# Opening of a linear-attention stage: sums and masks by halves of heads for two units, u asked first, head copies on GpSimd

## The chip, the cores and the metric

The kernel runs on one core of one Trainium2 chip. The metric is the device time of one execution in microseconds (us); several runs are made and their median is taken. The core's engines work side by side, each through its own queue in order: TensorE (PE: matrix products and transposes; PEld: its weight loads), VectorE (DVE), ScalarE (ACT), GpSimd (POOL) and SyncE (SP, which here only issues transfers). An engine whose next instruction waits does nothing else in the meantime.

## The reference

An attention block with a decaying state runs first, and its output is the input of a mixture-of-experts block. Sizes: batch B = 4, heads H = 8, sequence S = 768, head size D = 48; 3072 tokens of 384 numbers, 8 experts with a hidden size of 1024.

```
state = 0
for t in range(S):
    cur = (u * k_t) outer v_t
    y_t = r_t @ (state + cur)
    state = w * state + k_t outer v_t
x = y as (B*S, H*D)
logits = x @ w_gate; every token goes to one expert, at most N/E tokens each, best logits first
out[tokens of e] = relu(x @ w1[e]) @ w2[e]
```

The `cur` term gives each token's own contribution, the sum over d of r*u*k for each head, times v. It is needed at once by every tile of tokens, and the first steps of the kernel below prepare it.

## The kernel before, in words

**Units.** The attention stage cuts the sequence into 6 chunks of T = 128 tokens; a chunk of one batch element is a unit, 24 units in all, numbered with the batch element running fastest (units 0 to 3 are the first chunk). The program works in pairs of heads: four pairs `a`, each with a first and a second head `z`, on partitions 0 to 47 and 64 to 111. `head(a, z)` names the head; pairs 0 and 1 hold heads 0 to 3, pairs 2 and 3 hold heads 5, 6, 7 and 4. So head 4 is needed behind head 7, and a *head copy* (`again_one`, line 344; from unit 5 on `again`, line 340, for k and r together on VectorE) puts it there in the tile `krs`.

**What a unit needs.** Its k, r and v are loaded by SP (line 336, 192 KB each). `keys` (line 436, GpSimd) multiplies k by the table `wk`. `own` (lines 442 and 443, GpSimd) forms r*k, then times `u_bc`; `own_sum` (line 448, VectorE) sums it over d into `dd`, one number a head. `diagonal` (line 495, ScalarE) writes eight pieces of `AT`, the identity times `dd` of a head. `turn` transposes k and r on TensorE (line 458); the results are scaled or copied to `kT` and `rT` (lines 473 and 477 on VectorE, 475 on ScalarE). `pairs` forms k times r of all heads on TensorE into the PSUM tile `g_ps` (line 504), and VectorE copies those of earlier tokens over the diagonals in `AT` (line 508, `copy_predicated` with `mask`), one instruction for each `z`. `outputs` multiplies `AT` with v on TensorE (line 542), after the state's part (also line 542's helper) from the second chunk on; ScalarE copies the result (line 560). `keep` (lines 521 to 529) updates the state. `rows` transposes a unit's outputs back to rows (line 591), ScalarE copies them (line 598), SP stores them (line 599). `gate` and `logits` follow after each chunk.

**The order** is written out by hand: the whole stage stands in `tc.manual_schedule()`, so each engine runs its instructions as the program names them. Iteration n of the loop in `run` turns unit n + 2, forms the products of unit n + 1, the keys and own products of unit n + 3, and the outputs of unit n; it asks for k and r of unit n + 5 and v of unit n + 4. `krs` has 5 slots, `vts` 6, `AT` 3, `g_ps`, `y_ps`, `kT_ps` and `rT_ps` one each.

**The opening** (`start`, and `run` up to the loop) must in addition build the tables: powers of w on VectorE (lines 381 to 393), products of powers `Q` (line 395, one on GpSimd and one on VectorE), from these `WK` and `WR` on ScalarE (line 422), and `wk`, which is `WK` transposed on TensorE (line 427) and copied (line 431). u is one row, loaded by GpSimd's queue (line 364) behind the identity; a product with a row of ones spreads it over the partitions (line 409) and ScalarE copies it to `u_bc` (line 413). `idle` (line 418) issues transposes that nobody reads. Unit 0 is scaled straight from `Q` ("pieces"), units 1 and 2 by `WK` and `WR`.

After the attention stage come the assignment of tokens and the experts' products, which the change doesn't touch. The first expert's weights are loaded by SP (line 1506) near the end of the attention stage.

Of the kernel before, what the change touches and what calls it, by code (L numbers as in the profile page):

```python
# [10 lines left out]
F32 = mybir.dt.float32  # L11
# [5 lines left out]
ALU = mybir.AluOpType  # L17
AX = mybir.AxisListType
# [3 lines left out]
T = 128  # L22
# [252 lines left out]
class Mild:  # L275
# [65 lines left out]

    def again_one(self, n, x):
        t, HP, H, D = self.krs[:, n % self.NK, x], self.HP, self.H, self.D
        self.nc.scalar.copy(t[:, H, 0:D], t[:, HP, 0:D])

    def start(self):
        nc, HP, H, D = self.nc, self.HP, self.H, self.D
        half = HP // 2
        nc.vector.memset(self.wp, 1.0)
        with nc.allow_non_contiguous_dma(reason="a row to the partitions"):  # L350
            for eng, z, aa, hh in ((nc.sync, 0, slice(0, half), slice(0, HP, 2)),
# [4 lines left out]
                eng.dma_start(self.wp[z * PD:z * PD + D, aa], self.w[hh].rearrange("h d -> d h"))  # L356
        for n, what in ((0, "kr"), (1, "kr"), (0, "v"), (2, "kr"), (1, "v"), (3, "kr"), (2, "v"), (4, "kr"), (3, "v")):
            self.load(n, what)
        make_identity(nc, self.ident)
        nc.vector.memset(self.krs[:, :, :, :, D:PD], 0.0)  # L360
        AB = self.ones8
        nc.vector.memset(AB[:, :, :, :, 0:1], 1.0)
        nc.gpsimd.memset(self.wgp, 0.0)
        nc.gpsimd.dma_start(self.u_row, self.u.rearrange("h d -> (h d)").unsqueeze(0))
        nc.vector.memset(self.one_row, 1.0)
# [27 lines left out]
        nc.vector.reciprocal(AB[:, 1], AB[:, 0])  # L393
        for x, eng in ((0, nc.gpsimd), (1, nc.vector)):
            eng.tensor_mul(self.Q[:, x], AB[:, x, :, 1, :].unsqueeze(3).to_broadcast([128, HP, 9, 8]),
                           AB[:, x, :, 0, 0:8].unsqueeze(2).to_broadcast([128, HP, 9, 8]))
        Q = self.Q.rearrange("p x a i j -> p x a (i j)")
# [40 lines left out]

    def own(self, n):
        nc, H, D = self.nc, self.H, self.D  # L440
        rk = self.pool.tile([128, H, D], F32, name="rk")
        nc.gpsimd.tensor_mul(rk, self.krs[:, n % self.NK, 1, 0:H, 0:D], self.krs[:, n % self.NK, 0, 0:H, 0:D])  # L442
        nc.gpsimd.tensor_mul(rk, rk, self.u_bc)  # L443
        self.live[n].update(rk=rk)

    def own_sum(self, n):
        dd = self.pool.tile([128, self.H], F32, name="dd")
        self.nc.vector.tensor_reduce(out=dd, in_=self.live[n]["rk"], axis=AX.X, op=ALU.add)  # L448
        self.live[n]["dd"] = dd

# [35 lines left out]

    def diagonal(self, n, zs=(0, 1)):
        nc, HP = self.nc, self.HP
        if "AT" not in self.live[n]:
            self.live[n]["AT"] = self.pool.tile([128, 2, HP, T], F32, name="AT", bufs=3)  # L490
        AT, dd = self.live[n]["AT"], self.live[n]["dd"]
        for z in zs:
            for a in range(HP):
                h = self.head(a, z)
                nc.scalar.mul(AT[:, z, a, :], self.ident, dd[:, h:h + 1])  # L495

    def pairs(self, n, between=None):
        nc, HP, D = self.nc, self.HP, self.D
        kT, rT, AT = (self.live[n][x] for x in ("kT", "rT", "AT"))
        g_ps = self.ps.tile([128, 2, HP, T], F32, name="g_ps")  # L500
        for a in range(HP):
            for z in range(2):
                rows = slice(z * PD, z * PD + D)
                nc.tensor.matmul(g_ps[:, z, a, :], kT[rows, a, :], rT[rows, a, :], start=True, stop=True)  # L504
        if between is not None:
            between()
        for z in range(2):
            nc.vector.copy_predicated(out=AT[:, z], mask=self.mask.unsqueeze(1).to_broadcast([128, HP, T]),  # L508
                                      data=g_ps[:, z])

    def keep(self, n):
# [101 lines left out]
    def run(self, step):  # L613
        N, B, C, walk = self.N, self.B, self.C, self.walk
        self.live = {n: {} for n in range(N)}
        self.start()
        u_ps = self.spread_u()
        self.again_one(0, 0)
        k0 = self.keys_turned(0, True)
        self.again_one(0, 1)  # L620
        self.idle(2, "g_ps")
        r0 = self.r_turned(0)
        self.copy_u(u_ps)
        self.own(0)
        self.scaled(0, "k", k0, "pieces")
        self.scaled(0, "r", r0, "pieces")
        self.table(self.WK, "k")
        self.again_one(1, 0)
        self.table(self.WR, "r")
        self.again_one(1, 1)  # L630
        self.idle(2, "g_ps")
        k1 = self.keys_turned(1, True, walk.ps, "few")
        wk_ps = self.wk_turned()
        r1 = self.r_turned(1, walk.ps, "counts")
        self.wk_table(wk_ps)
        self.scaled(1, "k", k1, self.WK)
        self.own_sum(0)
        self.diagonal(0, (0,))
        self.again_one(2, 0)
        self.diagonal(0, (1,))  # L640
        self.again_one(2, 1)
        self.scaled(1, "r", r1, self.WR)
        self.own(1)
        self.keys(0)
        self.own_sum(1)
        nc, AB = self.nc, self.ones8
        nc.vector.tensor_mul(self.chunk, AB[:, 0, :, 1, 8], AB[:, 0, :, 1, 8])
        self.pairs(0)
        self.diagonal(1)
        self.own(2)  # L650
        chores = walk.constants()
        for n in range(N):
            self.load(n + 5, "kr")
            self.load(n + 4, "v")
            if n == 2:
                self.gate_weights()
            soon, split, full = n <= B, 0 < n < 3, n >= B and n % B == 0
            halves = ((0,), (1,)) if split or full else ((0, 1), ())
# [1221 lines left out]
```

## Time and profile before

| What | us |
|---|---|
| median of 3 runs (398.03 to 398.3) | 398.09 |
| profiled execution | 397.39 |
| its span | 395.7 |
| TensorE busy in the span | 381.1 |
| ScalarE busy | 162.0 |
| GpSimd busy | 138.4 |
| unit 0's k asked / turned on TensorE | 1.89 / 5.27 |
| unit 0's outputs on TensorE | 14.93 to 16.02 |
| copies of the outputs of units 0, 1, 2, 3, 4 (line 560) | 17.83, 21.20, 25.13, 30.22, 36.32 |
| the same of units 5, 6 | 41.02, 45.60 |
| last unit's copy | 124.70 |

In the lines of the profile, a timeline row gives the start, the duration, the engine, the line of the kernel, the operation, what is written from what, the shape, the count, and in brackets how long the engine had been idle and who released it. A row "x8" merges eight instructions, and its duration is that of all of them. The copies of line 560 serve as milestones, one for each unit.

### The profile page before, as it was taken

To read this page: it belongs to the slowest core of one execution; us is meant where nothing else is said; L and a number is where in the kernel's file an instruction comes from. 1 tells how busy PE (TensorE), PEld (TensorE's weight loads), DVE (VectorE), ACT (ScalarE), POOL (GpSimd) and SP (SyncE) were. 2 spreads that over 40 slices of the span, in tenths; PEclk is the share of its full clock that TensorE was granted. 3 is DMA by queue.
4 is the path that set the end of the run, shared out by engine and by line. 5 is a ranking of instruction groups with operands and counts; after the bars stand their busy time and mean duration, and the time that the engine had idled before them with its cause. 6 is when DMAs were issued, how large, how long until landed. Compare 5 with 4: busy or idle time off the path is not lost. (4 is left out here: it accounts for less than half of the span.)

```text
span 395.7 us, 8692 instructions
## 1 busy us (share of the span) xinstructions
PE 381.1 (96%) x3243; PEld 289.3 (73%) x3243; DVE 266.9 (67%) x934; ACT 162.0 (41%) x429; POOL 138.4 (35%) x173
## 2 busy tenths in 40 slices
PE   7899999999999999999999999999999999999993
PEld 5678888888877765587578569558757856966991
DVE  6755777576885677897839819979578663952630
ACT  4998888888873312222222122121222222222130
POOL 7888877666732013032121120302303211040020
PEclk9999999999999999999999999999999999999998
DMA  9999999898692155371460650109209173380010
GB/s 120 156 183 200 200 173 205 156 169 157 117 342 81 42 200 217 96 282 42 160 239 16 214 210 2 60 0 333 87 21 354 59 275 131 92 308 2 2 61 27
DMA packets 95331, 57.29 MB, mean 145 GB/s; under 512 B 77232, under 2 KB 89520, under 8 KB 95280
## 3 DMA queue, kind: packets, MB, share of 16 engines
q1 hardware_dynamic: 91936, 47.21, 47.7%
q0 software_dynamic: 3104, 9.44, 6.8%
q8 instruction: 27, 0.44, 0.5%
q14 instruction: 24, 0.20, 0.2%
q10 hardware_dynamic: 240, 0.00, 0.0%
HBM read 47.20 MB, written 9.44 MB: 143 GB/s over the span
## 5 line engine op out<-in xcount | busy, mean ns | idle before, releaser
L1541 PE MATMUL h_ps<-xT,w 128*128 128x384 f32 (+1 forms) x384 | 120.7, 467 | 0.6 <-ACT xT L1529 0.6
L1541 PEld LDWEIGHTS h_ps<-xT,w 128*128 128x128 f32 x384 | 66.4, 190 | 38.1 <-issue 2.5
L1543 ACT ACTIVATE hid<-h_ps 128x384 f32<-128x384 f32 (+1 forms) x64 | 29.7, 465 | 91.1 <-PE h_ps L1541 85.1
L495 ACT ACTIVATE AT<-ident,dd 128x128 f32<-128x128 f32 x192 | 59.6, 391 | 1.9 <-DVE dd L448 1.8
L1513 POOL DMA_INDIRECT xg<-x_rows,tok x22 | 22.4, 1017 | 95.6 <-PE h_ps L1541 32.1
L1637 POOL DMA_INDIRECT out_dram<-o_all,to x16 | 17.9, 1120 | 94.6 <-DVE o_all L1625 62.2
L508 DVE COPY_PREDICATED AT<-mask,g_ps 128x512 f32<-128x512 uint8 x48 | 32.6, 733 | 12.1 <-PE g_ps L504 10.6
L1620 ACT COPY res<-p_ps 128x384 f32<-128x384 f32 (+2 forms) x28 | 13.3, 474 | 60.5 <-PE p_ps L1616 60.5
L1643 PE MATMUL o_ps<-w,hid 128*128 128x384 f32 x96 | 33.1, 488 | 0.0
L504 PE MATMUL g_ps<-rT,kT 48*128 48x128 f32 x384 | 27.9, 284 | 0.7 <-DVE AT L508 0.6
L436 POOL TENSOR_TENSOR kss<-krs,wk 128x384 f32<-128x384 f32 x24 | 24.3, 1015 | 8.0 <-DVE krs L340 5.5
L504 PEld LDWEIGHTS g_ps<-rT,kT 48*128 48x128 f32 x384 | 23.4, 187 | 4.0 <-PE unread_ps L418 0.5
L542 PE MATMUL y_ps<-AT,vts 128*64 128x128 f32 x384 | 25.7, 276 | 0.0
L443 POOL TENSOR_TENSOR rk<-rk,u_bc 128x384 f32<-128x384 f32 x24 | 24.2, 1007 | 1.9
L442 POOL TENSOR_TENSOR rk<-krs 128x384 f32<-128x384 f32 x24 | 24.5, 1020 | 0.2 <-DMA krs<-in_r_dram 0.2
L1643 PEld LDWEIGHTS o_ps<-w,hid 128*128 128x128 f32 x96 | 17.2, 190 | 9.5 <-issue 0.2
L542 PEld LDWEIGHTS y_ps<-AT,vts 128*64 128x64 f32 x384 | 20.6, 137 | 1.2 <-issue 0.7
L1616 PE MATMUL p_ps<-T,S 128*128 128x192 f32 x120 | 20.9, 328 | 0.0
L1593 DVE TENSOR_TENSOR H<-hid 128x512 f32<-128x512 f32 x12 | 7.9, 686 | 19.1 <-ACT hid L1543 19.1
L1616 PEld LDWEIGHTS p_ps<-T,S 128*128 128x128 f32 x120 | 19.6, 190 | 0.1
L932 DVE TENSOR_TENSOR own<-counts,same 128x64 f32<-128x64 f32 x21 | 4.7, 222 | 21.7 <-PE counts L944 21.6
L1616 PE MATMUL p_ps<-w,hid 128*128 128x192 f32 (+1 forms) x112 | 19.0, 316 | 0.0
(303 smaller groups left out, 694.0 us busy)
## 6 DMA issues: line engine op xcount, KB each, us to landing
w<-in_moe_w_dram SPq DMA_DIRECT2D x18, 1536.0 KB, 10.2
krs<-in_k_dram SPq DMA_DIRECT2D x24, 192.0 KB, 4.0
krs<-in_r_dram SPq DMA_DIRECT2D x24, 192.0 KB, 4.7
vts<-in_v_dram SPq DMA_DIRECT2D x24, 192.0 KB, 4.7
x_rows<-xr SPq DMA_DIRECT2D x24, 192.0 KB, 3.2
xg<-x_rows,tok POOLq DMA_INDIRECT x22, 4.4
out_dram<-o_all,to POOLq DMA_INDIRECT x16, 2.8
out_dram<-o_sb,to POOLq DMA_INDIRECT x5, 3.0
```

What stands on the lines that cost most here:

```text
L436: self.nc.gpsimd.tensor_mul(self.kss[:, n % self.NS].rearrange("p (g h) d -> p g h d", g=2)[:, :, :, 0:D], src, self.wk.rearrange("p (g h) ...
L442: nc.gpsimd.tensor_mul(rk, self.krs[:, n % self.NK, 1, 0:H, 0:D], self.krs[:, n % self.NK, 0, 0:H, 0:D])
L443: nc.gpsimd.tensor_mul(rk, rk, self.u_bc)
L495: nc.scalar.mul(AT[:, z, a, :], self.ident, dd[:, h:h + 1])
L504: nc.tensor.matmul(g_ps[:, z, a, :], kT[rows, a, :], rT[rows, a, :], start=True, stop=True)
L508: nc.vector.copy_predicated(out=AT[:, z], mask=self.mask.unsqueeze(1).to_broadcast([128, HP, T]), data=g_ps[:, z])
L542: nc.tensor.matmul(yv[q * PD:(q + 1) * PD, o // 2, o % 2, :], lhsT, rhs, start=(o // 2, q) not in seen, stop=stop, skip_group_check=True)
L1513: nc.gpsimd.indirect_dma_start(out=xg[:, c, :], out_offset=None, in_=x_dram[0:within, :], in_offset=bass.IndirectOffsetOnAxis(ap=tok[:, c: ...
L1541: nc.tensor.matmul(h_ps[:, 0:m], w1[:, f, ts(j, 128)], xT[:, f, 0:m], start=(f == 0), stop=(f == KD - 1))
L1543: nc.scalar.activation(hid[:, j, 0:m], h_ps[:, 0:m], AF.Relu)
L1616: nc.tensor.matmul(ps[:, q, :], left[a][:, j, :], right[b][:, j, :], start=(j == 0), stop=(j == KF // 2 - 1))
L1643: nc.tensor.matmul(o_ps, hid[:, j, ts(c, 128)], w2[:, j, :], start=(j == 0), stop=(j == KF - 1))
```

## The change

It edits only the attention stage's opening and the placing of some instructions in its first five iterations.

- The load of u is issued on GpSimd's queue before the identity is made there, not behind it.
- Unit 2's k and r are asked ahead of unit 0's v, and so on down the list; inside the loop v is asked for unit n + 3, not n + 4.
- Both `Q` products are on VectorE.
- `own(0)` multiplies k by u first, then by r. For units 0 and 1 the second product of `own`, the sum, the diagonal and the mask are issued in two halves of heads (heads 0 to 3 and 4 to 7; a masked half covers pairs 0 and 1, or 2 and 3, with both `z`).
- Unit 0's first half of the diagonal comes between the two tables; its second half comes after `wk`. `wk` is turned after k and r of unit 1, ahead of unit 0's products. Unit 0's and unit 1's masks are interleaved with unit 1's sums.
- Unit 2's sum (`own_sum(2)`) and the chunk's factor come after unit 1's masks; before, the sum stood ahead of `pairs(1)` and the factor ahead of `pairs(0)`.
- The head copies of units 1 to 7 are on GpSimd (`gpsimd.tensor_copy`); for units 3 to 7 they stand directly before the `keys` and the `own` that use the same unit. Unit 0's stay on ScalarE.
- `own(2)` comes before `keys(0)`. One more idle transpose is issued ahead of unit 1's turn.

```diff
@@ again_one, start
-    def again_one(self, n, x):
+    def again_one(self, n, x, copy=None):
         t, HP, H, D = self.krs[:, n % self.NK, x], self.HP, self.H, self.D
-        self.nc.scalar.copy(t[:, H, 0:D], t[:, HP, 0:D])
+        (copy or self.nc.scalar.copy)(t[:, H, 0:D], t[:, HP, 0:D])
...
-        for n, what in ((0, "kr"), (1, "kr"), (0, "v"), (2, "kr"), (1, "v"), (3, "kr"), (2, "v"), (4, "kr"), (3, "v")):
+        for n, what in ((0, "kr"), (1, "kr"), (2, "kr"), (0, "v"), (3, "kr"), (1, "v"), (4, "kr"), (2, "v")):
             self.load(n, what)
+        nc.gpsimd.dma_start(self.u_row, self.u.rearrange("h d -> (h d)").unsqueeze(0))
         make_identity(nc, self.ident)
...
-        nc.gpsimd.dma_start(self.u_row, self.u.rearrange("h d -> (h d)").unsqueeze(0))
...
-        for x, eng in ((0, nc.gpsimd), (1, nc.vector)):
-            eng.tensor_mul(self.Q[:, x], ...
+        for x in range(2):
+            nc.vector.tensor_mul(self.Q[:, x], ...
@@ own, own_sum, diagonal, pairs
-    def own(self, n):
+    def own(self, n, u_first=False):
         nc, H, D = self.nc, self.H, self.D
+        k, r = (self.krs[:, n % self.NK, x, 0:H, 0:D] for x in range(2))
         rk = self.pool.tile([128, H, D], F32, name="rk")
-        nc.gpsimd.tensor_mul(rk, self.krs[:, n % self.NK, 1, 0:H, 0:D], self.krs[:, n % self.NK, 0, 0:H, 0:D])
-        nc.gpsimd.tensor_mul(rk, rk, self.u_bc)
+        if u_first:
+            nc.gpsimd.tensor_mul(rk, k, self.u_bc)
+        else:
+            nc.gpsimd.tensor_mul(rk, r, k)
+        for hs in self.parts(n):
+            nc.gpsimd.tensor_mul(rk[:, hs], rk[:, hs], r[:, hs] if u_first else self.u_bc[:, hs])
         self.live[n].update(rk=rk)
+    def parts(self, n):
+        H = self.H
+        return (slice(0, H // 2), slice(H // 2, H)) if n < 2 else (slice(0, H),)
+
+    def own_sum(self, n, part=0):
+        if "dd" not in self.live[n]:
+            self.live[n]["dd"] = self.pool.tile([128, self.H], F32, name="dd")
+        hs = self.parts(n)[part]
+        self.nc.vector.tensor_reduce(out=self.live[n]["dd"][:, hs], in_=self.live[n]["rk"][:, hs], axis=AX.X, op=ALU.add)
...
-    def diagonal(self, n, zs=(0, 1)):
+    def diagonal(self, n, zs=(0, 1), hs=range(99)):
...
-                nc.scalar.mul(AT[:, z, a, :], self.ident, dd[:, h:h + 1])
+                if h in hs:
+                    nc.scalar.mul(AT[:, z, a, :], self.ident, dd[:, h:h + 1])
...
-        for z in range(2):
+        for z in range(2) if n > 1 else ():
             nc.vector.copy_predicated(out=AT[:, z], ...
+        return g_ps
+
+    def masked_half(self, n, g_ps, i):
+        half = self.HP // 2
+        at = slice(i * half, (i + 1) * half)
+        mask = self.mask.unsqueeze(1).unsqueeze(1).to_broadcast([128, 2, half, T])
+        self.nc.vector.copy_predicated(out=self.live[n]["AT"][:, :, at], mask=mask, data=g_ps[:, :, at])
@@ run
         self.again_one(0, 0)
         k0 = self.keys_turned(0, True)
+        self.copy_u(u_ps)
+        self.own(0, True)
         self.again_one(0, 1)
         self.idle(2, "g_ps")
         r0 = self.r_turned(0)
-        self.copy_u(u_ps)
-        self.own(0)
+        self.own_sum(0, 0)
         self.scaled(0, "k", k0, "pieces")
+        self.own_sum(0, 1)
         self.scaled(0, "r", r0, "pieces")
         self.table(self.WK, "k")
-        self.again_one(1, 0)
+        self.diagonal(0, hs=first)
         self.table(self.WR, "r")
-        self.again_one(1, 1)
-        self.idle(2, "g_ps")
+        for x in range(2):
+            self.again_one(1, x, nc.gpsimd.tensor_copy)
+        self.idle(3, "g_ps")
         k1 = self.keys_turned(1, True, walk.ps, "few")
+        r1 = self.r_turned(1, walk.ps, "counts")
+        self.scaled(1, "k", k1, self.WK)
+        self.own(1)
+        self.scaled(1, "r", r1, self.WR)
         wk_ps = self.wk_turned()
-        r1 = self.r_turned(1, walk.ps, "counts")
         self.wk_table(wk_ps)
-        self.scaled(1, "k", k1, self.WK)
-        self.own_sum(0)
-        self.diagonal(0, (0,))
-        self.again_one(2, 0)
-        self.diagonal(0, (1,))
-        self.again_one(2, 1)
-        self.scaled(1, "r", r1, self.WR)
-        self.own(1)
+        self.diagonal(0, hs=second)
+        g0 = self.pairs(0)
+        self.masked_half(0, g0, 0)
+        self.own_sum(1, 0)
+        self.diagonal(1, hs=first)
+        self.masked_half(0, g0, 1)
+        self.own_sum(1, 1)
+        self.diagonal(1, hs=second)
+        for x in range(2):
+            self.again_one(2, x, nc.gpsimd.tensor_copy)
+        self.own(2)
         self.keys(0)
-        self.own_sum(1)
-        nc.vector.tensor_mul(self.chunk, AB[:, 0, :, 1, 8], AB[:, 0, :, 1, 8])
-        self.pairs(0)
-        self.diagonal(1)
-        self.own(2)
...
             self.load(n + 5, "kr")
-            self.load(n + 4, "v")
+            self.load(n + 3, "v")
...
             if n == 0:
                 self.turn(2, True)
+                self.idle(3, "y_ps")
+                g1 = self.pairs(1)
+                for i in range(2):
+                    self.masked_half(1, g1, i)
                 self.own_sum(2)
-                self.idle(3, "y_ps")
-                self.pairs(1)
+                nc.vector.tensor_mul(self.chunk, AB[:, 0, :, 1, 8], AB[:, 0, :, 1, 8])
                 self.keys(1)
...
-            if soon:
-                self.again_one(n + 3, 0)
             if n + 2 < N:
                 self.diagonal(n + 2, halves[0])
-            if soon:
-                self.again_one(n + 3, 1)
...
             if n + 3 < N:
+                if soon:
+                    self.again_one(n + 3, 0, nc.gpsimd.tensor_copy)
                 self.keys(n + 3)
+                if soon:
+                    self.again_one(n + 3, 1, nc.gpsimd.tensor_copy)
                 self.own(n + 3)
```

More of the change, by code (lines that the diff above doesn't have):

```diff
@@ L393, in start @@
         nc.vector.reciprocal(AB[:, 1], AB[:, 0])
-        for x, eng in ((0, nc.gpsimd), (1, nc.vector)):
-            eng.tensor_mul(self.Q[:, x], AB[:, x, :, 1, :].unsqueeze(3).to_broadcast([128, HP, 9, 8]),
-                           AB[:, x, :, 0, 0:8].unsqueeze(2).to_broadcast([128, HP, 9, 8]))
+        for x in range(2):
+            nc.vector.tensor_mul(self.Q[:, x], AB[:, x, :, 1, :].unsqueeze(3).to_broadcast([128, HP, 9, 8]),
+                                 AB[:, x, :, 0, 0:8].unsqueeze(2).to_broadcast([128, HP, 9, 8]))
         Q = self.Q.rearrange("p x a i j -> p x a (i j)")
@@ L437, in keys @@
                                   self.wk.rearrange("p (g h) d -> p g h d", g=2))
-    def own(self, n):
+    def own(self, n, u_first=False):
         nc, H, D = self.nc, self.H, self.D
+        k, r = (self.krs[:, n % self.NK, x, 0:H, 0:D] for x in range(2))
         rk = self.pool.tile([128, H, D], F32, name="rk")
-        nc.gpsimd.tensor_mul(rk, self.krs[:, n % self.NK, 1, 0:H, 0:D], self.krs[:, n % self.NK, 0, 0:H, 0:D])
-        nc.gpsimd.tensor_mul(rk, rk, self.u_bc)
-        self.live[n].update(rk=rk)
[L446 to L449, printed above, removed]
+        if u_first:
[4 more added lines that the diff above has]
+            nc.gpsimd.tensor_mul(rk[:, hs], rk[:, hs], r[:, hs] if u_first else self.u_bc[:, hs])
+        self.live[n].update(rk=rk)
+    def parts(self, n):
[6 more added lines that the diff above has]
+        self.nc.vector.tensor_reduce(out=self.live[n]["dd"][:, hs], in_=self.live[n]["rk"][:, hs], axis=AX.X, op=ALU.add)
     def pair(self, t, a):
@@ L616, in run @@
         self.start()
+        first, second = range(self.H // 2), range(self.H // 2, self.H)
+        nc, AB = self.nc, self.ones8
         u_ps = self.spread_u()
@@ L622, in run @@
         r0 = self.r_turned(0)
-        self.copy_u(u_ps)
-        self.own(0)
+        self.own_sum(0, 0)
         self.scaled(0, "k", k0, "pieces")
+        self.own_sum(0, 1)
         self.scaled(0, "r", r0, "pieces")
         self.table(self.WK, "k")
-        self.again_one(1, 0)
+        self.diagonal(0, hs=first)
         self.table(self.WR, "r")
-        self.again_one(1, 1)
-        self.idle(2, "g_ps")
+        for x in range(2):
+            self.again_one(1, x, nc.gpsimd.tensor_copy)
+        self.idle(3, "g_ps")
         k1 = self.keys_turned(1, True, walk.ps, "few")
+        r1 = self.r_turned(1, walk.ps, "counts")
+        self.scaled(1, "k", k1, self.WK)
+        self.own(1)
+        self.scaled(1, "r", r1, self.WR)
         wk_ps = self.wk_turned()
-        r1 = self.r_turned(1, walk.ps, "counts")
         self.wk_table(wk_ps)
-        self.scaled(1, "k", k1, self.WK)
-        self.own_sum(0)
-        self.diagonal(0, (0,))
-        self.again_one(2, 0)
-        self.diagonal(0, (1,))
-        self.again_one(2, 1)
-        self.scaled(1, "r", r1, self.WR)
-        self.own(1)
-        self.keys(0)
-        self.own_sum(1)
-        nc, AB = self.nc, self.ones8
-        nc.vector.tensor_mul(self.chunk, AB[:, 0, :, 1, 8], AB[:, 0, :, 1, 8])
-        self.pairs(0)
-        self.diagonal(1)
-        self.own(2)
+        self.diagonal(0, hs=second)
[9 more added lines that the diff above has]
+        self.own(2)
+        self.keys(0)
         chores = walk.constants()
```

## The prediction, made before the result was known

> **What bounds the kernel now.** I read the page's slices first (TensorE at 9 from the second slice on), then busy time by stretches, then the timeline of the first 37 us with the waits beside it.
>
> ```profile
> core 0: us, PE busy (x) PEld busy (x) DVE busy (x) ACT busy (x) POOL busy (x), PEclk, DMA share, GB/s
> 16.00:20.30 4.30, 4.04 (x68) 3.68 (x64) 3.17 (x6) 3.95 (x14) 2.88 (x4) 1.00 1.05 142
> 20.30:24.30 4.00, 3.99 (x62) 3.44 (x56) 1.27 (x4) 4.00 (x14) 3.92 (x5) 1.00 1.25 184
> 24.30:29.50 5.20, 4.34 (x61) 3.61 (x61) 3.71 (x8) 5.20 (x18) 4.25 (x5) 1.00 1.18 186
> ...
> 40.90:45.50 4.60, 4.60 (x79) 4.00 (x77) 3.40 (x8) 4.00 (x11) 4.38 (x9) 1.00 1.05 186
> ```
>
> One row is one unit's stretch: length, then busy us of each engine. From about 36 us on, TensorE is busy 4.60 of 4.60: a unit costs 4.58 us there, and nothing in that part is changed but the order of the v loads. So the change is worth what it moves the end of unit 4's outputs, 36.27 us now. Before that, ScalarE is the full engine (4.00 of 4.00, 5.20 of 5.20), with TensorE close behind it.
>
> ```profile
> 7.05 1.27 POOL L442 TENSOR_TENSOR rk<-krs 128x384 f32<-128x384 f32 x1
> 8.40 1.00 POOL L443 TENSOR_TENSOR rk<-rk,u_bc 128x384 f32<-128x384 f32 x1
> ...
> 11.47 0.55 DVE L448 TENSOR_REDUCE dd<-rk 128x8 f32<-128x384 f32 x1 [0.89 <-POOL rk L443]
> ...
> 14.77 0.54 DVE L448 TENSOR_REDUCE dd<-rk 128x8 f32<-128x384 f32 x1
> ...
> 15.23 1.36 DVE L508 COPY_PREDICATED AT<-mask,g_ps 128x512 f32<-128x512 uint8 x2
> 15.35 2.45 ACT L495 ACTIVATE AT<-ident,dd 128x128 f32<-128x128 f32 x8
> ...
> 17.83 0.57 ACT L560 COPY x<-y_ps 128x512 f32<-128x512 f32 x1
> ...
> 19.71 0.23 ACT L344 COPY krs<-krs 128x48 f32<-128x48 f32 x1
> ...
> 25.07 0.65 PE L458 MATMUL kT_ps<-ident,kss 128*112 128x128 f32 x4 [0.78 <-POOL kss L436]
> ...
> 30.22 0.60 ACT L560 COPY x<-y_ps 128x512 f32<-128x512 f32 x1
> ...
> 30.87 0.60 PE L591 MATMUL x_ps<-ident,x 112*128 112x112 f32 x4 [0.16 <-ACT x L560]
> ```
>
> The reader is to see a chain on ScalarE. Unit 2's sum (14.77) releases its diagonal at 15.35; eight pieces later comes the copy of unit 0's outputs (17.83), and from there ScalarE hardly pauses until the copy of unit 3's outputs at 30.22, which TensorE waits for at 30.87. TensorE then runs to 36.27 almost without a gap. Its waits between unit 0's and unit 4's outputs come to some 1.7 us.
>
> [...] The trace: 384 elements take 1.01 us and 192 (line 527) 0.51, so 2.6 ns an element[...]. [...] the product at 7.05, beside line 395 on VectorE (0.46 us, two SBUF inputs), took 1.27 instead of 1.00. [...] in the trace sums start 0.46 to 0.48 before the next instruction.
>
> **The change, part by part.** I laid the instructions of each engine in their written order, each starting when its engine is free and its inputs are there. Start-to-start times are from the timeline: diagonal piece 0.295, output copy 0.48, turned-key copy 0.47, row copy 0.37, head copy 0.13, half of a mask 0.65, scaling 0.60 (from pieces 0.67), unit's keys on GpSimd 0.97, own products 1.09 and 0.97. Laid for the old order, this puts unit 4's end at 36.23 (trace 36.27) and the copy at 30.22 at 30.32, so the method is good to about 0.1.
>
> *u first.* The issue on GpSimd's queue takes 0.71 us (line 364) and now stands ahead of the identity: that moves from 1.38 to 2.1, TensorE's twelve idle transposes (2.8 us) with it, and the spread of u ends at 5.8, not 5.1. Its copy still comes 0.8 earlier than now (5.8 for 6.59), since it no longer stands behind the copy for r. Unit 0's key turn slips from 5.27 to 5.8; that is free, as its scaling has something later to wait for.
>
> *Own products.* k times u starts at 6.3. It now lies beside both Q products on VectorE, so I add the 0.27 twice: 1.5 us (bounds: 1.0 with no collision, 1.7). The first half by r (0.5, as 192 elements) ends at 8.44.
>
> *VectorE's queue.* Q takes 0.42 more (ends 7.9). Then: half sum at 8.48 (0.28; bounds 0.22 and 0.35), keys 0.67, half sum 0.28, r 0.67, unit 1's keys and r 1.20: free at 11.58. Unit 0's products on TensorE stand behind the turn of wk, which waits for GpSimd's two head copies of unit 1 (to 9.3), and run 10.7 to 11.9. Each masked half reads both z, so I let it wait for all of them (bound: half of them, 0.3 earlier). From 11.91: mask 0.65, half sum 0.28, mask 0.65, half sum 0.28, unit 2's two scalings 1.20, unit 1's masks 1.30: free at 16.27. Only then comes unit 2's sum, which used to stand ahead of unit 1's masks: ready at 16.82, not 15.31.
>
> *ScalarE.* Unit 2's diagonal starts at 16.86 instead of 15.35; 2.36 later, at 19.22, the copy of unit 0's outputs, 1.39 later than now. Queued behind it are all of ScalarE's work for units 3 to 5, and TensorE itself, whose turn of unit 3 is done by 18.5 and whose transposes of unit 0's rows stand next: it waits some 1.4 us. The six head copies between the two output copies are gone: 6 times 0.125 gives back 0.75. So the copy of unit 3's outputs comes at 30.87, 0.65 later than in the trace and 0.55 later than the old order laid the same way.
>
> *TensorE.* It does gain at first: unit 1's products run 13.66 (13.84), unit 0's outputs 14.7 (14.93), unit 2's products 16.4 (16.74), and the 0.78 wait at 25.07 goes. The wait for the output copy takes all that. Unit 4's outputs end 0.5 later than in the old order.
>
> *Head copies on GpSimd.* Not in the trace there. Bounds: 0.11 (a memset of four elements, line 849) and 0.29 (a cast of 128 elements, line 375); I take 0.2. There are fourteen, and ten stand ahead of the end of unit 5's own products, which then comes at 27.1, as now. Its sum (0.6 with the hand-overs) is wanted by ScalarE at 28.5: a cover of 0.8 us, used up when the ten cost 0.28 each. Unit 0's keys move from 11.4 to 13.9 on that queue, behind unit 2's own products; the state's products on TensorE want them at 15.7.
>
> *Loads.* Each takes 1.2 us of the queue. Units 2 to 4 of k and r come one place earlier (1.2), v of unit 0 two later: landed at about 12.4, wanted at 14.7. The v loads go one iteration back, so v of unit 22 now stands behind the expert's weights on SP's queue; the present one there, issued at 107.62, landed 10.7 us later (the longest v), at 118.3; unit 22's outputs read it at 120.89. Cover 2.6 us, so nothing. Without it the end moves by what is missing. Unit 5's k waits for unit 0's keys to free its slot, at 14.8 in the new order; SP reaches that load only near 17 (18.37 in the trace).
>
> The turn of wk moves behind r of unit 1, and its copy on ScalarE from 9.0 to 10.9; GpSimd's keys want it at 13.9, so 3 us cover it. The extra idle transpose (0.12) lies in a wait; the chunk's factor (0.39) moves past unit 2's sum and is wanted by the first state, later.
>
> **Sum.** +0.5 us. The profiled execution took 397.39 us (span 395.7 and 1.7 around it); the median of the runs is 0.7 above it, 398.09. So 398.6.
>
> **Rivals.** *TensorE sets the pace.* If unit 2's diagonal started by about 15.0, the copy would never be waited for: outputs of unit 0 from 14.7 (0.25 earlier), and the 1.7 us of waits gone, up to 1.9 us less. For it: TensorE and GpSimd both have the work ready. Against: VectorE's queue has to be free 1.8 us earlier. With u at 5.1, the product at 1.27 and masks after half of the products, the sums give only -0.4 us. It passes 0.8 us only if several of my terms are too large together.
>
> *GpSimd becomes the bound.* If a head copy costs 0.35, ten of them put unit 5's own products at 28.6, past the 28.5 at which ScalarE wants them: ScalarE waits for the sum (0.55), and unit 3's output copy behind it moves. That gives +1.2 us; it decides from about 0.29 each. For it: GpSimd has no pause left from 6 to 33 us. Against: the nearest one-input rows are shorter.
>
> *Not what it says.* "u asked first" may bring no earlier u, since the identity waits behind it; that is already in the sum.
>
> **Numbers.** What a measurement of this kernel can tell from no change is about 0.2%, 0.8 us. Third diagonal late on ScalarE, 0.60: 0 to +1.0 us, of which 0.12 above 0.8. TensorE sets the pace, 0.22: 0.09 within 0.8 and 0.13 beyond it. GpSimd the bound, 0.18, all slower. So faster 0.13, same 0.57, slower 0.30. The range, 397.3 to 399.8, reaches from the middle of the first rival (-0.8) to past the second (+1.7, a copy at 0.4).
>
> **What would show it.** Right: unit 2's sum near 16.3 after unit 1's masks; TensorE waiting over 1 us for the first output copy (line 560's), near 19; no wait for kss at 25; the copy of unit 3's outputs between 30.3 and 31. Wrong: that copy before 29.9, a head copy on GpSimd of 0.29 or more, a wait for v near 120 us.

## The result, and the profile after

The changed kernel takes 399.53 us (median of 6 runs, 399.35 to 400.07) against 398.24 for the kernel before in the same session (6 runs, 398.03 to 398.58): the ratio is 1.0034, 95% interval 1.0024 to 1.0044, so it is slower by some 1.3 us. The forecast was 398.6, with a range of 397.3 to 399.8. The profiled execution took 399.35 us (span 397.5).

First, busy time by stretches. The columns are start and end, length, then the busy us of PE, PEld, DVE, ACT and POOL.

```profile
core 0: us, PE busy (x) PEld busy (x) DVE busy (x) ACT busy (x) POOL busy (x), PEclk, DMA share, GB/s
18.30:22.50 4.20, 3.08 (x46) 2.58 (x44) 2.85 (x5) 3.99 (x13) 4.04 (x7) 1.00 0.97 159
36.90:41.50 4.60, 4.60 (x79) 4.00 (x77) 2.65 (x6) 3.72 (x12) 3.87 (x9) 1.00 1.07 191
```

From about 37 us on TensorE is full again, 4.60 of 4.60. The loss is made ahead of that. In the first row TensorE is busy only 3.08 of 4.20, while ScalarE and GpSimd are both nearly full. The timeline shows the steps of the loss, here in order of time over all engines.

```profile
1.38 0.70 POOL L359 DMA_DIRECT2D u_row<-in_u_dram  x1 [0.86 <-POOLq L1892]
2.72 2.82 PE L418 MATMUL unread_ps<-ident 128*128 128x128 f32 x12 [2.72 <-POOL ident masks.py:199]
5.48 1.64 PE L409 MATMUL u_ps<-u_row,one_row 1*128 1x384 f32 x2
7.16 0.48 ACT L413 COPY u_bc<-u_ps 128x384 f32<-128x384 f32 x1 [1.83 <-PE u_ps L409]
7.72 1.20 POOL L444 TENSOR_TENSOR rk<-krs,u_bc 128x384 f32<-128x384 f32 x1 [2.01 <-ACT u_bc L413]
9.62 0.35 DVE L459 TENSOR_REDUCE dd<-rk 128x4 f32<-128x192 f32 x1 [1.56 <-POOL rk L448]
15.93 1.36 DVE L527 COPY_PREDICATED AT<-mask,g_ps 128x512 f32<-128x512 uint8 x2
17.20 0.52 DVE L459 TENSOR_REDUCE dd<-rk 128x8 f32<-128x384 f32 x1
17.76 2.45 ACT L506 ACTIVATE AT<-ident,dd 128x128 f32<-128x128 f32 x8 [1.40 <-DVE dd L459]
20.12 0.56 ACT L578 COPY x<-y_ps 128x512 f32<-128x512 f32 x1
20.73 0.60 PE L609 MATMUL x_ps<-ident,x 112*128 112x112 f32 x4 [1.11 <-ACT x L578]
31.73 0.57 ACT L578 COPY x<-y_ps 128x512 f32<-128x512 f32 x1
32.36 0.60 PE L609 MATMUL x_ps<-ident,x 112*128 112x112 f32 x4 [0.50 <-ACT x L578]
37.81 0.59 ACT L578 COPY x<-y_ps 128x512 f32<-128x512 f32 x1 [0.64 <-PE y_ps L560]
```

Two rows of the kernel before, beside them:

```profile
1.44 2.82 PE L418 MATMUL unread_ps<-ident 128*128 128x128 f32 x12 [1.44 <-POOL ident masks.py:199]
6.59 0.47 ACT L413 COPY u_bc<-u_ps 128x384 f32<-128x384 f32 x1
```

The reader is to see the forecast chain, later throughout. TensorE starts at 2.72 instead of 1.44, since it waits for the identity, and u is copied at 7.16, later than before (6.59), although it is asked first. Unit 2's sum stands right behind unit 1's masks (15.93, 17.20). ScalarE has been idle for 1.40 us when that sum comes; then it writes eight pieces of the diagonal before it copies unit 0's outputs at 20.12 (17.83 before). TensorE waits 1.11 us for that copy. Unit 4's copy is at 37.81 (36.32 before): +1.49. TensorE's waits up to 40 us changed as follows; the first three lines are of the kernel before, the others of the changed one.

```profile
PE kT_ps L458 <- DMA krs<-in_k_dram: 1.2, 3, 0.7
PE rT_ps L458 <- DMA krs<-in_r_dram: 0.9, 2, 0.5
PE kT_ps L458 <- POOL kss L436: 0.8, 1, 0.8
...
PE unread_ps L418 <- POOL ident masks.py:199: 2.7, 1, 2.7
PE x_ps L609 <- ACT x L578: 1.8, 3, 1.1
PE g_ps L515 <- DVE AT L527: 0.5, 1, 0.5
```

The columns are who waits for whom, the total, how often, and the longest; kss is what `keys` writes. The three waits of the kernel before are gone. In their place stand 1.3 more for the identity (2.7 for 1.4) and 1.6 more for output copies (1.8 for 0.2).

### The profile page after: what moved, and what is told of

It reads as the page before. It is cut to its first block, busy times and chain, and to the rows that moved or that the text cites. A ratio compares the mean times of both kernels' runs of the same rounds, so it can differ in the third digit from the quotient of the medians.

```text
span 397.5 us, 8681 instructions
## 1 busy us (share of the span) xinstructions
PE 382.8 (96%) x3244; PEld 291.6 (73%) x3244; DVE 268.2 (67%) x937; ACT 159.7 (40%) x415; POOL 139.4 (35%) x188
## 4 chain that ended last, share of the span: by engine, by line
PE 78%; DVE 8%; issue 4%; POOL 3%; ACT 3%; DMA 1%; POOLq 0%; another core or an unknown queue 0%; DVEq 0%
PE h_ps L1567 26%; PE p_ps L1642 14%; PE o_ps L1669 7%; PE y_ps L560 6%; PE g_ps L515 4%; PE e_h_ps L1737 3%; PE e_o_ps L1745 3%; PE kT_ps L468 2%; PE kv_ps L539 2%; PE x_ps L609 2%; PE rT_ps L468 2%; PE lg_ps L589 2%; DVE W L1619 1%; ACT AT L506 1%; DVE H L1619 1%
## 5 line engine op out<-in xcount | busy, mean ns | idle before, releaser
L519 DVE COPY_PREDICATED AT<-mask,g_ps 128x512 f32<-128x512 uint8 x44 | 30.0, 734 | 12.2 <-PE g_ps L515 11.2
L448 POOL TENSOR_TENSOR rk<-rk,u_bc 128x384 f32<-128x384 f32 (+1 forms) x24 | 23.3, 972 | 1.8
L446 POOL TENSOR_TENSOR rk<-krs 128x384 f32<-128x384 f32 x23 | 23.2, 1010 | 0.0
```

Source lines behind the costliest of these rows:

```text
L446: nc.gpsimd.tensor_mul(rk, r, k)
L448: nc.gpsimd.tensor_mul(rk[:, hs], rk[:, hs], r[:, hs] if u_first else self.u_bc[:, hs])
```

## The experiments

Every ratio is against the kernel before, run on the same chip in the same session. The milestones are the starts of the output copies of units 0, 3 and 4 in the profile.

| kernel | ratio, 95% interval | unit 0 | unit 3 | unit 4 |
|---|---|---|---|---|
| before | 1 | 17.83 | 30.22 | 36.32 |
| the change | 1.0034 (1.0024 to 1.0044) | 20.12 | 31.73 | 37.81 |
| a1_u_behind | 1.0005 (0.9999 to 1.0012) | 18.93 | 30.54 | 36.62 |
| b1_u_first_alone | 1.0023 (1.0012 to 1.0034) | 19.40 | 31.75 | 37.84 |
| a2_sum2_early | 1.0021 (1.0011 to 1.0030) | 18.87 | 31.36 | 37.42 |
| a3_both | 0.9995 (0.9987 to 1.0003) | 17.60 | 30.17 | 36.23 |
| c1_first_copy_ahead | 1.0016 (1.0008 to 1.0024) | 17.40 | 31.67 | 37.75 |
| c3_heads_back_on_scalar | 1.0052 (1.0038 to 1.0065) | 20.41 | 32.56 | 38.65 |
| c6_whole_sums | 1.0012 (1.0006 to 1.0019) | 19.31 | 30.92 | 36.99 |
| c2_best_heads_on_vector | 1.0030 (1.0017 to 1.0043) | 17.58 | 31.27 | 37.35 |
| c7_three_engines_mended | 0.9987 (0.9980 to 0.9994) | 18.11 | 30.04 | 36.11 |

One profile is one execution, and TensorE's pace in the opening differs between executions (see the section on d0 and d1 below), by up to 0.6 us at these milestones. So where two kernels are within that, the ratio decides. A ratio is known to 0.0007 to 0.0013 (0.3 to 0.5 us), so a difference between two of them only to some 0.4 to 0.7 us.

### The order of u: a1 and b1

a1 puts the load of u back where it was in the changed kernel. b1 moves it forward in the kernel before, and nothing else.

```diff
 # a1, against the changed kernel (b1 is the opposite edit of the kernel before)
-        nc.gpsimd.dma_start(self.u_row, self.u.rearrange("h d -> (h d)").unsqueeze(0))
         make_identity(nc, self.ident)
...
         nc.gpsimd.memset(self.wgp, 0.0)
+        nc.gpsimd.dma_start(self.u_row, self.u.rearrange("h d -> (h d)").unsqueeze(0))
```

> The changed kernel with one edit: u is issued behind the identity and the gate's zeros again, as before. Theory (the late u): the issue ahead of the identity puts the twelve idle transposes at 2.72 instead of 1.44, TensorE then runs its first products at half rate, the copy of u comes at 7.2 and all of VectorE's queue 1.1 to 1.7 us late. Undone: unit 0's first half sum at 7.9 to 8.1 (9.62), unit 2's diagonal near 16.3 (17.76), unit 3's output copy near 30.3 (31.73), time within 0.3 us of the kernel before, 1.1 to 1.7 below the changed one. Rival (the rest of the new order costs it: GpSimd with head copies and halves, or the v loads behind the weights): at most 0.4 us of the 1.3 come back.

> The kernel before with one edit of the change alone: u is issued ahead of the identity. Theory: the identity comes 1.3 us late and TensorE runs slow up to about 10 us, unit 0's r is turned near 8.4 to 9.4 instead of 6.48, its mask starts near 13.4 instead of 12.34, unit 2's diagonal near 16.7 instead of 15.35; time 1.0 to 1.5 us above the kernel before. Rival (u's place is free, as unit 0's sum is wanted late): within 0.3 us of the kernel before.

a1: 397.78 us for 397.69, no measurable difference from before. b1: 398.92 for 397.69. So "u asked first" costs 1.15 us in the changed kernel (0.0029 of 398) and 0.9 in the old one. In a1's profile TensorE starts at 1.44, the first half sum is at 8.43, and every milestone from unit 0 to unit 4 is 1.19 earlier than in the change: what the opening loses is never won back. a1's first products ran as slowly as the change's (1.64 us for the spread of u; from start to start, four transposes take 0.86 us at 7.08 and 0.44 at 9.40, so about half rate), against what was expected of the slow pace, so these 1.19 come from the order and not from the pace.

b1's ten runs fall into two groups: three take 397.75 to 397.9 us, as the kernel before, and seven take 398.84 to 399.22. The profiled execution (398.98) is of the second group and has the slow pace. Whether the first group had the fast pace is not shown, so the 0.9 us is a mean of two cases.

### The place of unit 2's sum: a2, a3 and c1

```diff
 # a2, against the changed kernel (a3: with a1's edit as well)
                 self.turn(2, True)
+                self.own_sum(2)
                 self.idle(3, "y_ps")
...
                     self.masked_half(1, g1, i)
-                self.own_sum(2)
```

> The changed kernel with one edit: unit 2's sum stands ahead of unit 1's masks again. Theory (ScalarE's chain hangs on that sum): its diagonal starts near 16.5 instead of 17.76, the first output copy near 18.9 instead of 20.12, TensorE's wait for it shrinks from 1.11 to 0.3 or less, unit 3's output copy 0.6 earlier; time 0.5 to 0.8 us below the changed kernel, still 0.5 to 0.8 above the one before. Rival (the start of the queues alone sets the end, this order is hidden): no change against the changed kernel, within 0.2.

> Both edits together: u behind the identity, unit 2's sum ahead of unit 1's masks. Theory: the two add up until GpSimd's own products of unit 5 (end near 27) set unit 5's diagonal: unit 2's diagonal near 15.0, first output copy near 17.4, unit 3's output copy near 29.9; time 0.3 to 0.6 us below the kernel before. Rival (head copies on GpSimd cost more than they save): at or above the kernel before.

a2's sum comes at 15.93, its copy of unit 0's outputs 1.25 earlier, unit 4's only 0.39 earlier; in time it gains 0.5 us on the change, which is no more than the two intervals leave open. a3 gains 0.4 us on a1, run in the same session (397.36 for 397.78), which points the same way. a3 itself is at 0.9995, no difference from before, where 0.3 to 0.6 us below was expected. Between unit 0's copy and unit 4's, what was won shrinks, because GpSimd has become the late engine. Two rows of a3's timeline, and its waits on TensorE up to 45 us:

```profile
26.19 1.00 POOL L448 TENSOR_TENSOR rk<-rk,u_bc 128x384 f32<-128x384 f32 x1
27.81 2.45 ACT L506 ACTIVATE AT<-ident,dd 128x128 f32<-128x128 f32 x8 [0.38 <-DVE dd L459]
```

```profile
PE g_ps L515 <- DVE AT L527: 1.0, 2, 0.5
PE kT_ps L468 <- POOL kss L436: 0.8, 1, 0.8
PE x_ps L609 <- ACT x L578: 0.5, 1, 0.5
```

GpSimd ends unit 5's own products at 27.2, after working without a pause since 13.8, and ScalarE now waits for their sum. This is the mechanism of the rival "GpSimd becomes the bound". It does not act in the changed kernel, where ScalarE begins unit 5's diagonal without a pause (29.38, right behind the row copy), but it stands right behind ScalarE.

c1 leaves the sum where the change has it, and lets ScalarE copy unit 0's outputs ahead of unit 2's diagonal.

```diff
+            if n == 0:
+                self.outputs(0, lambda: step(0, "states"))
             if n + 2 < N:
                 self.diagonal(n + 2, halves[0])
...
-            self.outputs(n, lambda: step(n, "states"))
+            if n > 0:
+                self.outputs(n, lambda: step(n, "states"))
```

> The changed kernel with the copy of unit 0's outputs (and those outputs on TensorE) ahead of unit 2's diagonal in ScalarE's order. Theory (late third diagonal, with the copy queued behind it): ScalarE's 1.40 us of idle time ahead of the diagonal takes the copy, it starts near 17.0 instead of 20.1, TensorE no longer waits for x at unit 0's rows, unit 2's diagonal starts within 0.4 of 17.8, and unit 4's output copy comes at about 37.3 instead of 37.8; time 0.4 to 0.7 below the changed kernel, still 0.6 to 1.0 above before, since the diagonal itself stays late. Rival (TensorE's wait for the copy is the whole loss): unit 4's output copy at 36.7 and the time equal to before.

```profile
14.38 2.45 ACT L506 ACTIVATE AT<-ident,dd 128x128 f32<-128x128 f32 x8 [0.45 <-DVE dd L459]
17.40 0.58 ACT L578 COPY x<-y_ps 128x512 f32<-128x512 f32 x1 [0.56 <-PE y_ps L560]
18.23 2.45 ACT L506 ACTIVATE AT<-ident,dd 128x128 f32<-128x128 f32 x8 [0.25 <-DVE dd L459]
```

In c1's timeline of ScalarE the copy fills the pause, 2.7 us earlier than in the change. TensorE's wait for output copies falls from 1.8 to 0.7 in all. The ratio is 1.0016, 0.7 us below the change and 0.6 above before, as the theory had it. (The milestone of unit 4 missed its number: unit 1's diagonal is already 0.47 later than in the change's profile, by TensorE's slower opening.) So taking the wait away wins about half of the loss (0.7 of 1.3, give or take 0.5). The other half stays while the copy is early; unit 2's diagonal is then still at 18.23.

### The head copies: c3, c2

```diff
 # c3, against the changed kernel; units 1 and 2 stay on GpSimd
+            if soon:
+                self.again_one(n + 3, 0)
             if n + 2 < N:
                 self.diagonal(n + 2, halves[0])
+            if soon:
+                self.again_one(n + 3, 1)
...
-                if soon:
-                    self.again_one(n + 3, 0, nc.gpsimd.tensor_copy)
                 self.keys(n + 3)
-                if soon:
-                    self.again_one(n + 3, 1, nc.gpsimd.tensor_copy)
```

> The changed kernel with the head copies of units 3 to 7 back on ScalarE, around each unit's diagonal as before (units 1 and 2 stay on GpSimd). The prediction gave the move 0.75 us: six copies of 0.125 between the copy of unit 0's outputs and that of unit 3's. So here the distance between these two is 0.7 longer than in the changed kernel (11.61), unit 4's output copy comes at about 38.5, and the time is 0.6 to 0.8 above the changed kernel. Rival (GpSimd, with head copies of 0.19, sets the pace of these units): no change or a gain.

The stretch between unit 0's and unit 3's copies is 12.15 us instead of 11.61, so the six copies cost 0.54 there, not quite 0.75. TensorE's waits change: those for output copies fall from 1.8 to 0.3, and 0.9 for a head copy that stands behind the late diagonal and 0.8 for kss take their place. The time is 0.7 us above the change, as expected, so the move to GpSimd is worth about 0.7, though the two intervals leave nearly all of 0 to 1.4 open.

c2 starts from a3 and takes the copies of units 4 to 7 off GpSimd as well.

```diff
-                if not soon and n + 3 < N:
+                if n + 3 < N:
                     self.again(n + 3)
...
-                if soon:
+                if n == 0:
                     self.again_one(n + 3, 0, nc.gpsimd.tensor_copy)
 # the same for self.again_one(n + 3, 1, ...)
```

> u asked behind the identity, unit 2's sum ahead of unit 1's masks, and the head copies of units 4 to 7 on VectorE, one instruction for k and r at the start of the iteration (those of units 0 to 3 as in the change). Where both corrections were made, ScalarE waited 0.38 us for unit 5's sum, as GpSimd's products were late: four copies of 0.19 less ahead of them take that wait away. Expected unit 3's output copy at 29.7 to 30.0 (30.17 with both corrections), unit 4's at 35.7 to 36.0, time 0.4 to 0.9 below before. Rival: VectorE's copies push the masks, and nothing is gained over both corrections (within 0.2 of them).

c2 misses its number: 398.53 us, 0.3% above before, and worse than its rival said.

```profile
16.35 0.74 DVE L689 TENSOR_TENSOR chunk<-ones 128x4 f32<-128x4 f32 x1
19.32 0.21 DVE L340 COPY krs<-krs 128x96 f32<-128x96 f32 x1 [2.24 <-DMA krs<-in_r_dram]
19.45 0.35 DVE L547 TENSOR_TENSOR states<-kv_ps,chunk 128x192 f32<-128x192 f32 x1
19.71 1.34 DVE L519 COPY_PREDICATED AT<-mask,g_ps 128x512 f32<-128x512 uint8 x2
```

The 0.21 us copy stands at the head of VectorE's queue before unit 4's r has landed. VectorE waits 2.24 us for the transfer, and unit 2's masks, which start at 17.89 in a3, start at 19.71. Neither the theory nor its rival had asked when r lands.

### Halves of heads: c6

```diff
 # against a1
-        return (slice(0, H // 2), slice(H // 2, H)) if n < 2 else (slice(0, H),)
+        return (slice(0, H),)
...
-        self.own_sum(0, 1)
...
-        self.own_sum(1, 1)
```

> The changed kernel with u behind the identity, and without the halves: units 0 and 1 have one second own product of 384 elements and one sum of 8 heads, as before. If the halves are worth what the queue of VectorE says: the product ends 0.5 later (first sum at about 8.9 instead of 8.43) and a whole sum takes 0.2 more than half of one, so unit 0's scalings start 0.7 later; two half sums of 0.27 go; unit 2's sum comes 0.3 to 0.5 later, unit 4's output copy at 36.9 to 37.1 (36.62 with halves), time 0.2 to 0.5 above that kernel. Rival (the halves only fill a wait that is there anyway): within 0.1.

1.0012 against a1's 1.0005: 0.3 us, and unit 4's copy 0.37 later, both as expected. But the intervals of the two ratios overlap (0.9999 to 1.0012 and 1.0006 to 1.0019), and c6's profile had TensorE's fast opening and a1's the slow one, so a worth of the halves of about 0.3 us is likely and not shown. Two half sums take VectorE longer than a whole one (in a1 0.53 for unit 0's two, at 8.43 and 9.36, and 0.45 for unit 2's whole one, at 15.99, from start to start); what they could win is that the first comes early (unit 0's diagonal starts at 8.85 in a1 and at 9.28 in c6).

### TensorE's pace in the opening: d0 and d1

d0 is the kernel before and d1 the changed one, each profiled a second time.

> The kernel before, unchanged, profiled once more, for TensorE's pace in its opening. In the profile of before the spread of u took 0.91 us and four transposes 0.65 from 4.2 us on; in the five profiles of the other kernels the spread took 1.64 and the four transposes 1.1 until between 9.4 and 10.7. If that pace belongs to the kernel's order (late identity, later work), this profile shows 0.91 and 0.65 again. If it belongs to the execution or the chip, it shows 1.64 and 1.1 with the same instructions, the copy of u some 0.5 later or hidden behind the copy for r, and unit 4's output copy near 36.3 to 36.9.

> The changed kernel once more, profiled, for two things. TensorE's pace in the opening: if it belongs to this kernel's late identity, the spread of u takes 1.64 us and four transposes 1.1 again; if it differs from one execution to the next, some execution shows 0.9 and 0.65. And the last output copy: in the first profile it came at 127.30, 1.1 later than the shift of 1.48 that all units from 5 on had; if that belongs to the execution, it comes near 126.2 here.

The spread of u and the first turn of k, in five executions: before, d0, a1, c6, and d1. a1 and c6 give TensorE the same instructions up to here, and both start at 1.44.

```profile
4.19 0.91 PE L409 MATMUL u_ps<-u_row,one_row 1*128 1x384 f32 x2
5.27 0.65 PE L458 MATMUL kT_ps<-ident,krs 128*112 128x128 f32 x4 [0.18 <-DMA krs<-in_k_dram]
```

```profile
4.19 0.98 PE L409 MATMUL u_ps<-u_row,one_row 1*128 1x384 f32 x2
5.31 0.66 PE L458 MATMUL kT_ps<-ident,krs 128*112 128x128 f32 x4
```

```profile
4.19 1.64 PE L409 MATMUL u_ps<-u_row,one_row 1*128 1x384 f32 x2
5.76 1.10 PE L468 MATMUL kT_ps<-ident,krs 128*112 128x128 f32 x4
```

```profile
4.20 1.09 PE L409 MATMUL u_ps<-u_row,one_row 1*128 1x384 f32 x2
5.30 0.65 PE L468 MATMUL kT_ps<-ident,krs 128*112 128x128 f32 x4
```

```profile
5.48 1.64 PE L409 MATMUL u_ps<-u_row,one_row 1*128 1x384 f32 x2
7.06 1.10 PE L468 MATMUL kT_ps<-ident,krs 128*112 128x128 f32 x4
...
10.72 1.06 PE L468 MATMUL rT_ps<-ident,krs 128*112 128x128 f32 x4
```

Four transposes take 0.65 or 1.10 us for the same instructions. In a1 the slow pace lasts until about 9.4, in the change's first profile until about 10.5; in d1 r of unit 1 still takes 1.06 at 10.72, and all its milestones are 0.59 later than in the first profile of the same kernel (unit 4: 38.40 for 37.81). a1 and c6 show that the same instructions can meet either pace: it is not fixed by the order. But d0 repeats the fast pace of the kernel before, with its milestones within 0.02, and d1 the slow pace of the changed one, and that is what was expected if the order decides. In all, three of eight profiled executions with TensorE's start at 1.44 had the fast pace (before, d0, c6), and none of the six that start at 2.72 (the change, d1, a2, b1, c1, c3). So whether the late identity makes the slow pace likelier stays open.

What sets the pace is not shown. The faster pace sets in from about 3 us (before, c6) to about 9 us (d1) after the first transposes. a1 worked without a pause from 1.44 to 8.5 us (busy 5.20 of 5.20 from 4.2 to 9.4) and was still slow, while the kernel before, busy 4.30 of the same 5.20 us, was fast. The granted clock of the profile is 1.00 from 4.2 to 12.5 us in before, the change, a1, c6 and d1 alike, so it doesn't tell the two paces apart.

d1 also answers the second question. Its last output copy is at 127.87 where the shift of 2.06 gives 126.76: 1.1 late again, as in the first profile. c6 shows the same, a1, a3 and b1 don't. The copy of the logits behind it is only 0.3 later. The cause is open.

### Spread over three engines: c5 and c7

```diff
 # c7, against a3
-        for hs in self.parts(n):
+        for hs in self.parts(n) if n not in (4, 5) else ():
             nc.gpsimd.tensor_mul(rk[:, hs], ...
@@ own_sum
+        if n in (4, 5):
+            self.nc.vector.tensor_mul(self.live[n]["rk"], self.live[n]["rk"], self.u_bc)
@@ rows_out
-            nc.scalar.copy(xr, ...
+            (nc.vector.tensor_copy if n < 3 else nc.scalar.copy)(xr, ...
@@ run
-                self.keys(1)
...
                     self.keep(n - 1)
+                    if n == 1:
+                        self.own_sum(n + 2)
                     self.pairs(n + 1)
-                    if n != 2 and n + 3 < N:
+                    if n > 2 and n + 3 < N:
                         self.own_sum(n + 2)
...
                 self.own(n + 3)
-                if n == 1:
-                    self.keys(2)
+                if n < 2:
+                    self.keys(n + 1)
 # c5: keys(1) at n == 0, keys(2) at n == 2
```

> Both corrections (u behind the identity, unit 2's sum ahead of unit 1's masks), and the load of units 3 to 5 spread anew: the keys of unit 1 behind unit 3's own products and those of unit 2 behind unit 5's on GpSimd, unit 3's sum ahead of unit 2's masks, the second own product of units 4 and 5 on VectorE, and the row copies of units 0 to 2 on VectorE instead of ScalarE. With both corrections alone GpSimd has no pause from 13.8 to 30.6 us, TensorE waits 0.8 for unit 5's keys and 0.5 for unit 3's output copy, ScalarE 0.38 for unit 5's sum. If GpSimd is what holds that order back, both waits on TensorE go: unit 5's keys 1.0 earlier (22.9), unit 4's output copy at 35.1 to 35.6 (36.23 with both corrections), time 0.6 to 1.2 below before. Rival (VectorE, with three more copies and two products, becomes the late one): unit 4's copy at 36.2 or later and no gain.

In c5 unit 2's keys stand behind the load that reuses their slot, so they take unit 7's k: this kernel computes something else there, GpSimd waits 5.48 us for that load, and its time (404.69) says nothing. Up to that wait it shows unit 5's diagonal at 26.65, against 27.81 in a3.

> The spreading over three engines once more, with unit 2's keys back behind unit 4's own products, ahead of the load that reuses their slot. In the kernel with them behind unit 5's, unit 5's diagonal started at 26.65 (27.81 with both corrections alone) before TensorE waited 4.7 us for unit 2's keys, which waited for unit 7's load. Without that wait: unit 5's keys end near 23.9, ahead of TensorE's turn at 24.4; unit 5's diagonal stays at 26.6 to 26.9, unit 3's output copy at 29.0 to 29.3, unit 4's at 35.0 to 35.4 (36.23), and the time is 1.0 to 1.5 below before (0.9962 to 0.9975). Rival (what is won comes back as a wait of TensorE for units 6 or 7, whose loads and own products are not earlier): a wait for kss or for the mask between 29 and 45, unit 5's output copy at 40.5 or later (40.93), and the time within 0.5 of before.

c7 takes 397.26 us for 397.72: ratio 0.9987 (0.9980 to 0.9994), a gain of 0.5 us, less than the 1.0 to 1.5 expected. Both waits of TensorE are gone, and a new one of 0.6 for rT at 25.82 stands in their place. The numbers of the rival came out (unit 5's copy at 40.80, the time within 0.5 of before), but not its mechanism: TensorE waits neither for kss nor for the mask between 29 and 45 us. Unit 5's diagonal starts at 27.69, 1.04 later than in c5. c7's slower opening accounts for 0.29 of that (unit 0's copy 18.11 for 17.82). For the rest there is this:

```profile
21.73 1.35 DVE L460 TENSOR_TENSOR rk<-rk,u_bc 128x384 f32<-128x384 f32 x1 [0.52 <-POOL rk L446]
23.12 0.55 DVE L461 TENSOR_REDUCE dd<-rk 128x8 f32<-128x384 f32 x1
...
26.15 0.92 DVE L460 TENSOR_TENSOR rk<-rk,u_bc 128x384 f32<-128x384 f32 x1
27.10 0.55 DVE L461 TENSOR_REDUCE dd<-rk 128x8 f32<-128x384 f32 x1
```

```profile
21.65 1.02 POOL L436 TENSOR_TENSOR kss<-krs,wk 128x384 f32<-128x384 f32 x1
22.60 0.57 POOL L344 COPY krs<-krs 128x48 f32<-128x48 f32 x1
...
25.64 1.02 POOL L436 TENSOR_TENSOR kss<-krs,wk 128x384 f32<-128x384 f32 x1
```

The product on VectorE took 0.56 and 0.54 us in c5. The first of these began 0.21 us ahead of GpSimd's keys (21.71 and 21.92), which then took 1.21; the second met no work of GpSimd. In c7 the products begin 0.08 and 0.51 us behind the keys that they meet and take 1.35 and 0.92. Each ends 0.41 us after these keys (23.08 after 22.67, 27.07 after 26.66), and GpSimd's head copy behind the keys takes 0.57 and 0.56 instead of 0.23. Why they take longer side by side is not shown. The products are 0.8 and 0.4 us longer than in c5, and ScalarE waits 0.52 us for unit 5's sum behind the second. That this is what keeps c7 from the expected gain is argued; no run takes the meeting away. c7 has the lowest ratio of these kernels, and the only interval that lies below before; from a3 (0.9987 to 1.0003) it can't be told apart.

## Why the prediction was right, and where it was off

**Right: the chain.** Unit 2's sum stands behind unit 1's masks, its diagonal and the output copy come late, and TensorE waits for the copy. The forecast wait was 1.4 us and the profile's is 1.11; the stretch from unit 0's copy to unit 3's was to be 11.65 us and is 11.61 (12.39 before); a head copy on GpSimd was to take 0.2 us and takes 0.19 to 0.24. There is no wait for kss and none for v, as forecast. c1 supports the chain by taking the copy out of it. a2 and a3 move the sum; the copy is then 1.25 and 1.33 us earlier (a3 against a1), while the 0.4 to 0.5 us that they gain are hardly clear of noise. c3 supports the gain that was set against the loss.

**Not as forecast: the times in it.** Unit 2's sum comes at 17.20 and not near 16.3, the first output copy at 20.12 and not near 19, and unit 3's at 31.73, outside its "between 30.3 and 31". The result is slower by more than the 0.8 us that can be told from no change. The prediction gave that 0.30, against 0.57 for "same", and +1.3 lies beyond the 0 to +1.0 of its own leading case. The time lies in the range because the range also held the second rival. By its number alone the result would fit that rival (+1.2) better than the forecast (+0.5); it is the profile that excludes the rival, with head copies of 0.2 us and no pause of ScalarE ahead of unit 5's diagonal. So that the time fell in the range was in part luck.

**Off: the term for u.** The forecast let it bring the copy of u 0.8 earlier than before; it came 0.57 later. Its third rival named the danger and took it to be in the sum, but at too small a size. The identity is ready at 2.67 and not at 2.1, since GpSimd starts the issue of u at 1.38 and not at 0.8: +0.57. The spread then takes 1.64 us instead of 0.91: +0.73. So u is copied at 7.16, not 5.8. The product by u takes 1.20 instead of 1.5, which gives back 0.3, and the first half sum is at 9.62 for 8.48: +1.14. From there VectorE's queue kept its laid distances to 0.1 or 0.2 (a half sum, 0.28 by the author's estimate, takes 0.27 from start to start, 9.62 to 9.89), and the whole rest runs about 0.9 later than laid (unit 0's copy 20.12 for 19.22, unit 3's 31.73 for 30.87). Between the two profiles that covers the difference at unit 4, +0.5 laid and +1.49 measured.

In the medians (+0.5 forecast, +1.3 measured) only the first part is certain: the late identity (0.57) is in all six profiled executions that ask u first. The second part is from TensorE's pace. The sum rested on one profile of the kernel before, with the fast pace and 0.7 us below the median of its runs, and took that distance for a constant. Both profiles of before had the fast pace and both of the change the slow one; how often each kernel meets which is not known, so how much of the 0.73 is in the medians stays open.

This also shifts the weight of the causes. The forecast put the whole loss on the late sum and booked u as a gain. In the runs u first is the larger part (+1.15 by a1), and the late sum the smaller one.

**Rivals.** "TensorE sets the pace" did not come; its first condition, u at 5.1, is met by no kernel here that asks u first. a3 comes to its second, unit 2's diagonal at about 15.2 (half of the sixteen pieces that start at 12.72), and there GpSimd takes the gain. "GpSimd becomes the bound" did not come at 0.2 a copy, but a3 shows that it is the next bound; in c7 the late instruction is VectorE's, beside GpSimd's keys.

**What the parts are worth,** in us: u first +1.15, unit 2's sum late +0.4 to +0.5, head copies -0.7, halves -0.3, each to some 0.4 to 0.7. Only the first is well clear of that. These add up to +0.6, and the change measures +1.3. The remainder (both Q products on VectorE, the place of wk, the order of loads, that parts need not add, and noise) was not separated.

## What to carry to other kernels

A short instruction put first on a queue can delay everything that the queue feeds (here the issue of u, 0.70 us long and begun at 1.38, moved TensorE's start from 1.44 to 2.72): ask what stood there before it, here the identity on which all of TensorE waits. Where one engine is relieved, look for the engine that ends next and for when its inputs land, before moving more work: c2 lost about 1.4 us against a3 with a 0.2 us copy that stood ahead of its transfer, and c7 kept half or less of what was expected (0.5 us of 1.0 to 1.5), where VectorE's products met GpSimd's keys and took 1.35 and 0.92 us. And a forecast of half a per cent needs the profile's execution placed among its runs, since one trace can hold a lucky opening.

## What was not expected of the hardware

TensorE's opening pace differs by a factor of 1.7 for the same instructions (0.65 and 1.10 us for four transposes), ends between 4.5 and about 12 us, and goes with milestones of one kernel 0.59 us apart. A product of two SBUF operands on VectorE took 0.56 us in c5, begun 0.21 us ahead of GpSimd's keys, and 1.35 in c7, begun 0.08 us behind them. And an instruction that only issues a transfer, put first on GpSimd's queue, starts at 1.38 us after 0.86 of idle time, where the identity's memset in the same place starts at 0.81 in the kernel before.
